# Summing the first values on VectorE instead of TensorE, and a tile's exponentials ahead of the weight decoding on ScalarE

## The chip, the cores and the metric

One NeuronCore of a Trainium2 chip runs the whole program. Five engines read instruction streams of their own, each in order: TensorE (PE, matmuls; PEld its weight loads), VectorE (DVE), ScalarE (ACT), GpSimd (POOL) and SyncE (SP, which issues the DMAs here). The metric is the device time of one execution in microseconds, the median of several runs. Less is better.

## The reference

Attention over pooled keys and values, then two feed-forward layers on its output of 4608 tokens by 512 (8 batches of 576 tokens; hidden width 2048; all float32).

```python
k_p = k.reshape(B, H, Sp, pool, D).mean(axis=3)      # B 8, H 8, Sp 72, pool 8, D 64
v_p = v.reshape(B, H, Sp, pool, D).mean(axis=3)
scores = scale * np.matmul(q, k_p.transpose(0, 1, 3, 2))
scores = scores - np.max(scores, axis=-1, keepdims=True)
attn = np.exp(scores)
attn = attn / (np.sum(attn, axis=-1, keepdims=True) + 1e-09)
x = np.matmul(attn, v_p)                             # then to (4608, 512)
...
h = x @ w_in                                         # layer 1
x2 = (h * np.clip(h + 3.0, 0.0, 6.0) / 6.0) @ w_out
h = x2 @ w_in2                                       # layer 2: a rational function of h, then
out = g @ w_out2
```

The weights are handed over as the 64-bit words of float64, and the kernel decodes them on the chip.

## The kernel before

**Slots.** The program is one list of slots, written out by `slot(s)`. Slots -12 to -1 are the prologue; slots 0 to 143 each compute one of the 16 hidden blocks of one of 9 token groups of layer 1 (`hidden`, 12 matmuls into `ps_h`), slots 144 to 287 the same of layer 2. The output matmuls of a block (`out1`, 12 matmuls into `ps_y`) come two slots later. The attention of the next token group is spread over the slots of the present one. Every instruction stands on its engine in the order in which `slot` writes it; nothing reorders it later.

**Layer 1 between the two matmuls.** `hard_swish_a` writes tile `r` on ACT from `ps_h` (L453) and finishes it on DVE (L454). `hard_swish_b`, at the start of the next slot, splits it: `gh` on ACT (L460) and `gl` on POOL (L461). There is one buffer of `r`, two each of `gh`, `gl` and `ps_h`.

**Attention of a tile of up to 128 queries.** Scores on PE into a PSUM bank `ps_s` (L333); the highest score on DVE, `nm` (L348); the exponentials on ACT (L355, four L358, L361), which read the bank for the last time; the reciprocal `rc` on DVE (L369); `s` scaled on POOL (L370, L376); transposes on PE (L385); `pth` and `ptl` (L396, L397); and after a group of tiles the product with the values, `ps_v` (L414). From the second token group on, scores, transposes and products take turns in two banks, `a0` and `a1`, so each waits for the last reader of what stood in the bank two turns ago. The highest score of a tile is written in the slot `s_s` of its scores; its exponentials (the list `ex`) in slot `s_s + 1`, right behind `hidden`.

**Weights.** A chunk of 128 by 512 weights is decoded by `decode_a` and `decode_r` on ACT (L154, L159), `decode_b` on DVE (L173, L174 into `t`) and `decode_c` on POOL (L181), and then split in two parts: the high part on ACT (`w`, L201), the low part, which reads the high one, on DVE or, for every fourth chunk, on POOL (L203). One chunk is decoded in a prologue slot, three in two slots from slot 0 on; the 32 chunks of layer 1 are done in slot 14. Within a slot the lists come as `c2` (split), `c1` (decode_b and c, from chunk 24 on the whole of a chunk), `c3` (decode_a and r of a chunk of the next slot), `la`.

**Values.** `v` comes as 6 chunks of 128 rows by 8 times 64, to be summed over the 8. For batch 0 that is `pool_first_v`: eight matmuls a chunk with the identity, into one bank, two chunks a slot in slots -11 to -9; the tiles are named after their buffers, so the first is `k_raw`. For the other batches it is `pool_v` on DVE (L248). `split_v` then makes `vsh` on ACT (L287) and the rest on DVE (L288), and POOL masks them (L297).

```python
        for h in ahead(s):
            hidden(h)
        for f in ex.get(s, ()):
            f()
        if 0 <= s - 1 < T1:
            hard_swish_b(s - 1)
...
        for kind in (c2, c1, c3, la):
            for f in kind.get(s, ()):
                f()
```

Of the kernel before, what the change touches and what calls it, by code (L numbers as in the profile page):

```python
# [19 lines left out]
F32 = mybir.dt.float32  # L20
# [4 lines left out]
AF = mybir.ActivationFunctionType  # L25
ALU = mybir.AluOpType
AX = mybir.AxisListType

B, H, S, D = 8, 8, 576, 64
POOLED = 8  # L30
SP = S // POOLED
NT, DM, DFF = B * S, H * D, 2048
P = 128
# [8 lines left out]
VCH = 6  # L42
# [26 lines left out]
def feed_forward_kernel(tc, q_t, k_t, v_r, vmask, w_in1, w_out1, w_in2, w_out2, a_rep, b_rep, out):  # L69
    nc = tc.nc  # L70
# [7 lines left out]
    att = tc.alloc_tile_pool(name="att", bufs=1, side="right")  # L78
    dram = tc.alloc_tile_pool(name="spill", bufs=1, space=bass.MemoryType.DRAM)
    ps_y = tc.alloc_tile_pool(name="ps_y", bufs=1, space=bass.MemoryType.PSUM)  # L80
# [7 lines left out]
    ident = const.tile([P, P], F32, name="ident")  # L88
# [153 lines left out]
    vsum = {}  # L242
# [23 lines left out]
            dst = kbd[rows, :, j, SM:SP] if p == NPAIR else kbd[rows, p, j, 0:SM]  # L266
            nc.vector.tensor_reduce(out=dst, in_=k[rows], axis=AX.X, op=ALU.add)

    def pool_first_v(c):
        if c == 0:  # L270
            vsum[0] = ps_y.tile([P, 512], F32, tag="y0", name="ps_vs")
        for r in range(POOLED):
            nc.tensor.matmul(
                vsum[0][:, c * D:(c + 1) * D], lhsT=ident, rhs=v_raw[0, c][:, r, :],
                start=r == 0, stop=r == POOLED - 1,
            )

    vparts = {}

    def split_v(b):  # L280
        src = vsum.pop(b)
        vs = src
        if b == 0:
            src = src[:, 0:VCH * D].rearrange("p (c d) -> p c d", d=D)
            vs = att.tile([P, VCH, D], F32, tag="vsum", name="vsum")
        vsh = att.tile([P, VCH, D], F32R, tag="vsh", name="vsh")
        nc.scalar.activation(out=vsh, in_=src, func=AF.Copy)  # L287
        nc.vector.tensor_tensor(  # L288
            out=vs[:, 0:4, :], in0=src[:, 0:4, :], in1=vsh[:, 0:4, :].bitcast(F32), op=ALU.subtract
        )  # L290
        vparts[b] = vsh.bitcast(F32), vs, src

    def mask_v(b, f, part):
        src, dst, nm = vparts[b][part], (vh, vl)[part], ("vh", "vl")[part]
# [9 lines left out]

    def mask_rest(b):

        hi, vs, src = (x[:, 4:6, :] for x in vparts[b])
        nc.vector.tensor_scalar(out=hi, in0=hi, scalar1=mask[:, 3:4], scalar2=None, op0=ALU.mult)
        nc.vector.scalar_tensor_tensor(
            out=vs, in0=src, scalar=mask[:, 2:3], in1=hi, op0=ALU.mult, op1=ALU.add  # L310
        )
        for i in range(2):
            nc.vector.tensor_scalar(
                out=vr[:, :, i, 1, :], in0=vs, scalar1=mask[:, 4 + i:5 + i], scalar2=None, op0=ALU.mult
            )
# [253 lines left out]
    def at(kind, slot, f, *a):  # L569
        kind.setdefault(slot, []).append(lambda: f(*a))  # L570
# [5 lines left out]
    def prepare_first(s0, units):  # L576

        at(dm, s0, load_q, *units[0])
        for p in (0, 1, NPAIR):
            at(dm, s0, load_first_k, p)  # L580
        at(dm, s0, load_weights, 0, *chunks[0])
        for u in units[1:3]:
            at(dm, s0, load_q, *u)
        for p in (2, 3):
            at(dm, s0, load_first_k, p)
        for c in range(VCH):
            at(dm, s0, load_v, 0, c)
            at(pe, s0 + 1 + c // 2, pool_first_v, c)
        at(dm, s0, load_weights, 0, *chunks[1])
        for p in (0, NPAIR, 1):  # L590
            at(el, s0, pool_first_k, p)
        for p in (2, 3):
            at(la, s0 + p - 2, pool_first_k, p)
        at(la, s0 + 3, split_v, 0)
        for i in range(4):
            at(la, s0 + 4 + i // 2, mask_v, 0, i // 2, i % 2)
        at(la, s0 + 4, mask_rest, 0)
# [19 lines left out]
    for j in range(NB):  # L617
        s0 = MF * (j - 1)
        tail, head = ([(b, g, f, ti) for f in range(2) for ti in GROUPS[b][g][2]] if 0 <= b < B else []
                      for b, g in ((j - 1, 1), (j, 0)))  # L620
        units = tail + head
        groups = [[u for u in units if u[0::2] == k] for k in dict.fromkeys(u[0::2] for u in units)]
        steps = len(units) + len(groups)
        k, done, last_s = 0, {}, {}
        for us in groups:
            b, g, f, _ = us[0]
            for u in us + [None]:
                s = s0 + round(14 * k / (steps - 1)) if j else k + 2 - PRE
                k += 1
                if u is None:  # L630
                    done[b, f] = s
                    for i in range(2):
                        at(pe, s, attend, b, g, f, i)
                        at(mid, s, split_x, b, g, 2 * f + i)
                    continue
                ti = u[3]
                s_t.append(s)
                s_s = s_t[-3] if len(s_t) > 2 else len(s_t) - 1 - PRE
                last_s[b, f] = s_s
                if len(s_t) > 3:  # L640
                    at(dm, s_s - 2, load_q, *u)
                at(pe, s_s, scores, *u)
                at(hi, s_s, highest, b, f, ti)
                at(ex, s_s + 1, exponentials, b, f, ti)
                at(nz, s_s + 1, normalize, b, f, ti)
                at(pe, s, transposes, *u)
                at(mid, s, split_p, *u)
        if j == 0:
            prepare_first(-PRE, units)
        elif head:  # L650
            k0 = last_s[j - 1, 0] + 1
            k1 = max(last_s[j - 1, 1] + 1, k0 + 2)
            a0 = max(done[j - 1, 0], done[j, 0] - 4)
            a1 = max(done[j - 1, 1], done[j, 0] - 3)
            prepare(j, k0, k1, a0, a1)
# [72 lines left out]
    def slot(s):  # L728
        d = s - LAG
        if s < 0:  # L730
            for kind in (dm, ld, el, pe, hi, ex, nz, c1, mid, c2, c3, la):
                for f in kind.get(s, ()):
                    f()
            return
        for f in dm.get(s, ()):
            f()
        for h in ahead(s):
            hidden(h)
        for f in ex.get(s, ()):
            f()  # L740
        if 0 <= s - 1 < T1:
            hard_swish_b(s - 1)
        for kind in (el, ld, pe):
            for f in kind.get(s, ()):
                f()
        if T1 <= s < T2:
            rational_a(s)
        if d > T1 and d % MF == 0:
            evac2((d - T1) // MF - 1)
        if 0 <= d < T1:  # L750
            out1(d)
        elif T1 <= d < T2:
            out2(d)
        for kind in (nz, mid, hi):
            for f in kind.get(s, ()):
                f()
        if 0 <= s < T1:
            hard_swish_a(s)
        if 0 <= d < T1 and d % MF == MF - 1:
            evac1(d // MF)  # L760
        if T1 <= s - 1 < T2:
            rational_c(s - 1)
        for kind in (c2, c1, c3, la):
            for f in kind.get(s, ()):
                f()
        if d == T1 - 1:
            to_second_left()
        if T1 <= s < T2:
            rational_b(s)
# [73 lines left out]
```

## Time and profile before

| | |
|---|---|
| three runs | 1771.32, 1772.97, 1776.14 us; median 1772.97 us |
| the profiled execution | 1775.16 us, of which its span 1773.4 us |
| busy share of the span | PE 97%, PEld 80%, ACT 56%, DVE 55%, POOL 51% |
| chain that ended last | PE 89% (L447 42%, L552 22%, L472 21%, L333 2%, L414 2%, L385 1%) |
| mean granted TensorE clock | 0.986 of full |

The span is the time from the first to the last instruction of the core; the 1.8 us beside it lie around the program. A busy share says how long an engine had work; which engine the others wait for is read from the rows of the stretch in question, with the idle time in front of an instruction and what ended it.

### The profile page before, as it was taken

To read this page: it belongs to the slowest core of one execution; us is meant where nothing else is said; L and a number is where in the kernel's file an instruction comes from. 1 tells how busy PE (TensorE), PEld (TensorE's weight loads), DVE (VectorE), ACT (ScalarE), POOL (GpSimd) and SP (SyncE) were. 2 spreads that over 40 slices of the span, in tenths; PEclk is the share of its full clock that TensorE was granted. 3 is DMA by queue.
4 is the path that set the end of the run, shared out by engine and by line. 5 is a ranking of instruction groups with operands and counts; after the bars stand their busy time and mean duration, and the time that the engine had idled before them with its cause. 6 is when DMAs were issued, how large, how long until landed. Compare 5 with 4: busy or idle time off the path is not lost.

```text
span 1773.4 us, 22277 instructions
## 1 busy us (share of the span) xinstructions
PE 1722.7 (97%) x7824; PEld 1426.9 (80%) x7824; DVE 982.8 (55%) x1617; ACT 992.6 (56%) x2226; POOL 907.8 (51%) x888
## 2 busy tenths in 40 slices
PE   6697999999999999999999999999999999999999
PEld 6575888888888888888888888888888888888887
DVE  5874534536354453533211566666666666666665
ACT  5765445555555454545322566666666666666665
POOL 3564333434334343433223666666666666666665
PEclk9798999999999999999999999999999999999999
DMA  6541303323232323312045301010101010101000
GB/s 206 165 137 58 107 20 114 114 83 132 77 131 91 123 85 105 117 66 87 12 149 208 113 13 41 7 42 7 42 7 42 7 42 7 42 7 42 1 24 25
DMA packets 68336, 128.33 MB, mean 72 GB/s; under 512 B 11392, under 2 KB 27776, under 8 KB 68224
## 3 DMA queue, kind: packets, MB, share of 16 engines
q1 hardware_dynamic: 68224, 126.91, 21.5%
q8 instruction: 62, 1.02, 0.2%
q14 instruction: 50, 0.41, 0.1%
HBM read 91.23 MB, written 35.65 MB: 72 GB/s over the span
## 4 chain that ended last, share of the span: by engine, by line
PE 89%; DVE 0%; ACT 0%; POOL 0%; issue 0%; DVEq 0%
PE ps_h L447 42%; PE ps_o L552 22%; PE ps_y L472 21%; PE ps_s L333 2%; PE ps_v L414 2%; PE ps_t L385 1%; ACT s L358 0%; POOL gl L538 0%; DVE t L514 0%; DVE g L529 0%; DVE r L525 0%; DVE qd L522 0%; DVE t L513 0%; ACT y L478 0%; ACT o L560 0%
## 5 line engine op out<-in xcount | busy, mean ns | idle before, releaser
L461 POOL TENSOR_TENSOR gl<-r,gh 128x512 fp32r<-128x512 f32 x144 | 186.9, 1298 | 470.3 <-ACT gh L460 463.4
L472 PE MATMUL ps_y<-gh,w 128*128 128x512 f32 x1152 | 393.4, 403 | 0.0
L447 PE MATMUL ps_h<-xh,w 128*128 128x512 f32 x1152 | 378.9, 390 | 0.0
L447 PE MATMUL ps_h<-x2h,w 128*128 128x512 f32 x1152 | 377.8, 389 | 0.8 <-DVE t L514 0.8
L552 PE MATMUL ps_o<-w,gh 128*128 128x512 f32 x1152 | 354.6, 389 | 0.0
L472 PEld LDWEIGHTS ps_y<-gh,w 128*128 128x128 f32 x1152 | 220.0, 191 | 47.4 <-issue 1.6
L447 PEld LDWEIGHTS ps_h<-x2h,w 128*128 128x128 f32 x1152 | 216.4, 188 | 46.3 <-DVE t L514 1.2
L447 PEld LDWEIGHTS ps_h<-xh,w 128*128 128x128 f32 x1152 | 216.5, 188 | 45.1
L552 PEld LDWEIGHTS ps_o<-w,gh 128*128 128x128 f32 x1152 | 216.2, 188 | 44.9
L509 POOL TENSOR_SCALAR qd<-ah,coef 128x512 f32<-128x512 f32 x144 | 111.4, 774 | 234.1 <-ACT ah L507 234.1
L472 PE MATMUL ps_y<-gl,w 128*128 128x512 f32 x576 | 227.4, 395 | 0.0
L447 PE MATMUL ps_h<-xl,w 128*128 128x512 f32 x576 | 224.1, 389 | 0.0
L447 PE MATMUL ps_h<-x2l,w 128*128 128x512 f32 x576 | 224.1, 389 | 0.0
L552 PE MATMUL ps_o<-w,gl 128*128 128x512 f32 x576 | 224.1, 389 | 0.0
L522 DVE SCALAR_TENSOR_TENSOR qd<-qd,r 128x512 f32<-128x512 f32 x144 | 99.0, 687 | 220.1 <-ACT r L521 203.8
L538 POOL TENSOR_TENSOR gl<-g,gh 128x512 fp32r<-128x512 f32 x144 | 186.4, 1295 | 19.2 <-ACT gh L537 19.0
L512 POOL TENSOR_TENSOR qd<-qd,ah 128x512 f32<-128x512 f32 x144 | 187.0, 1299 | 12.0
L454 DVE SCALAR_TENSOR_TENSOR r<-r,ps_h 128x512 f32<-128x512 f32 x144 | 99.0, 688 | 169.6 <-ACT r L453 167.1
L507 ACT ACTIVATE ah<-ps_h 128x512 f32<-128x512 f32 x144 | 86.1, 598 | 152.0 <-PE ps_h L447 152.0
L453 ACT ACTIVATE r<-ps_h,cst 128x512 f32<-128x512 f32 x144 | 98.7, 685 | 111.0 <-PE ps_h L447 76.3
L520 ACT ACTIVATE r<-qd,cst 128x512 f32<-128x512 f32 x144 | 99.6, 692 | 105.0 <-POOL qd L512 104.9
L460 ACT ACTIVATE gh<-r 128x512 fp32r<-128x512 f32 x144 | 90.1, 625 | 104.4 <-PE ps_y L472 101.9
(87 smaller groups left out, 2575.9 us busy)
## 6 DMA issues: line engine op xcount, KB each, us to landing
raw<-w_in SPq DMA_DIRECT2D x32, 512.0 KB, 3.7
raw<-w_out SPq DMA_DIRECT2D x32, 512.0 KB, 3.7
w<-raw SPq DMA_DIRECT2D x32, 512.0 KB, 2.8
w<-w SPq DMA_DIRECT2D x32, 512.0 KB, 4.1
v_raw<-v_r SPq DMA_DIRECT2D x47, 256.0 KB, 4.0
y<-y SPq DMA_DIRECT2D x36, 256.0 KB, 2.9
x2r<-y SPq DMA_DIRECT2D x36, 256.0 KB, 2.9
out<-o SPq DMA_DIRECT2D x36, 256.0 KB, 2.2
```

The source lines that it names most:

```text
L447: nc.tensor.matmul(ps, lhsT=w, rhs=x, start=o == 0, stop=o == len(ops) - 1)
L453: nc.scalar.activation(out=r, in_=ps, func=AF.Relu, bias=cst[:, 0:1], scale=1.0 / 6.0)
L454: nc.vector.scalar_tensor_tensor(out=r, in0=r, scalar=1.0, in1=ps, op0=ALU.min, op1=ALU.mult)
L460: nc.scalar.activation(out=gh[it], in_=r, func=AF.Copy)
L461: nc.gpsimd.tensor_tensor(out=gl[it], in0=r, in1=gh[it].bitcast(F32), op=ALU.subtract)
L472: nc.tensor.matmul(yp[j][c], lhsT=w, rhs=x, start=m == 0 and o == 0, stop=m == MF - 1 and o == 2)
L509: nc.gpsimd.tensor_scalar(out=qd, in0=ah, scalar1=absb[1], scalar2=absb[0], op0=ALU.mult, op1=ALU.add)
L512: nc.gpsimd.tensor_tensor(out=qd, in0=qd, in1=ah, op=ALU.mult)
L520: nc.scalar.activation(out=r0, in_=qd, func=AF.Ln, scale=2.0 ** -LN_SHIFT, bias=cst[:, 1:2])
L522: nc.vector.scalar_tensor_tensor(out=qd, in0=qd, scalar=1.0 + 1e-6, in1=r0, op0=ALU.add, op1=ALU.mult)
L538: nc.gpsimd.tensor_tensor(out=gl[it], in0=g, in1=gh[it].bitcast(F32), op=ALU.subtract)
L552: nc.tensor.matmul(yp[j][c], lhsT=w, rhs=x, start=m == 0 and o == 0, stop=m == MF - 1 and o == 2)
```

## The change

Two parts. The values of batch 0 are summed by `pool_v` on VectorE, as those of the other batches are: six reductions written at the end of slots -11, -10 and -9, two in each; `pool_first_v` with its 48 matmuls is gone, and `split_v` and `mask_rest` read the sums from SBUF instead of a PSUM bank. And the exponentials of a tile whose scores are in slot 0 or later are written at the end of that same slot, ahead of the lists `c2`, `c1`, `c3` and `la`, instead of in the next slot behind `hidden`. In the prologue they stay where they were.

```diff
-    def pool_first_v(c):
-        if c == 0:
-            vsum[0] = ps_y.tile([P, 512], F32, tag="y0", name="ps_vs")
-        for r in range(POOLED):
-            nc.tensor.matmul(
-                vsum[0][:, c * D:(c + 1) * D], lhsT=ident, rhs=v_raw[0, c][:, r, :],
-                start=r == 0, stop=r == POOLED - 1,
-            )
...
     def split_v(b):
-        src = vsum.pop(b)
-        vs = src
-        if b == 0:
-            src = src[:, 0:VCH * D].rearrange("p (c d) -> p c d", d=D)
-            vs = att.tile([P, VCH, D], F32, tag="vsum", name="vsum")
+        vs = vsum.pop(b)
...
-            at(pe, s0 + 1 + c // 2, pool_first_v, c)
+            at(la, s0 + 1 + c // 2, pool_v, 0, c)
...
-                at(ex, s_s + 1, exponentials, b, f, ti)
+                at(ex, s_s if s_s >= 0 else s_s + 1, exponentials, b, f, ti)
...
         for h in ahead(s):
             hidden(h)
-        for f in ex.get(s, ()):
-            f()
...
-        for kind in (c2, c1, c3, la):
+        for kind in (ex, c2, c1, c3, la):
             for f in kind.get(s, ()):
                 f()
```

`pool_v` itself is not changed:

```python
    def pool_v(b, c):
        if c == 0:
            vsum[b] = att.tile([P, VCH, D], F32, tag="vsum", name="vsum")
        vr = v_raw.pop((b, c)).rearrange("p r d -> p d r")
        nc.vector.tensor_reduce(out=vsum[b][:, c, :], in_=vr, axis=AX.X, op=ALU.add)
```

Where it moves rows (the changed kernel is shorter, so its L320 is the old L333, and so on), first on PE in the prologue. Before, from the first scores on (`ps_vs` are the sums of the values):

```order
L333 MATMUL ps_s<-kbd,q_sb 128x144 x4
L273 MATMUL ps_vs<-k_raw,ident 128x64 x8
L273 MATMUL ps_vs<-v_raw,ident 128x64 x8
L385 MATMUL ps_t<-ident,s 128x128 x3
L333 MATMUL ps_s<-kbd,q_sb 128x144 x2
L273 MATMUL ps_vs<-v_raw,ident 128x64 x16
L385 MATMUL ps_t<-ident,s 128x128 x3
```

And after:

```order
L320 MATMUL ps_s<-kbd,q_sb 128x144 x4
L372 MATMUL ps_t<-ident,s 128x128 x3
L320 MATMUL ps_s<-kbd,q_sb 128x144 x2
L372 MATMUL ps_t<-ident,s 128x128 x3
L320 MATMUL ps_s<-kbd,q_sb 128x144 x2
```

The 48 matmuls are gone, and the transposes and scores of the prologue follow each other directly.

On DVE the same sums come in, here those of slots -11 and -10, after the change:

```order
L174 SCALAR_TENSOR_TENSOR t<-d,t 128x512
L248 TENSOR_REDUCE vsum<-k_raw 128x64
L248 TENSOR_REDUCE vsum<-v_raw 128x64
L267 TENSOR_REDUCE kbd<-k_raw 64x64 x2
L335 TENSOR_REDUCE nm<-ps_s 128x4
L356 RECIPROCAL rc<-sm 128x4
L173 TENSOR_SCALAR t<-d 128x512
L174 SCALAR_TENSOR_TENSOR t<-d,t 128x512
L384 TENSOR_TENSOR ptl<-ps_t,pth 128x2x128
L388 TENSOR_TENSOR pth<-ps_t,pth 32x128
L203 TENSOR_TENSOR w<-t,w 128x512
L248 TENSOR_REDUCE vsum<-v_raw 128x64 x2
```

Before, the same rows stand there without the three of L248: two reductions have come in behind the decoding of slot -11, two behind the split of slot -10, and two more (not shown) behind that of slot -9.

The second part, on ACT in slot 2 (`raw` is a chunk of weights being decoded). Before:

```order
L453 ACTIVATE r<-ps_h,cst 128x512
L201 ACTIVATE w<-t 128x512
L154 ACTIVATE raw_673<-raw_673 128x512
L159 ACTIVATE raw_673<-raw_673 128x512
L355 ACTIVATE nm<-nm 128x4
L358 ACTIVATE s,sm<-ps_s,nm 128x72 x4
L361 ACTIVATE sm<-sm,cst 128x4
L460 ACTIVATE gh<-r 128x512
```

And after:

```order
L440 ACTIVATE r<-ps_h,cst 128x512
L342 ACTIVATE nm<-nm 128x4
L345 ACTIVATE s,sm<-ps_s,nm 128x72 x4
L348 ACTIVATE sm<-sm,cst 128x4
L201 ACTIVATE w<-t 128x512
L154 ACTIVATE raw_630<-raw_630 128x512
L159 ACTIVATE raw_630<-raw_630 128x512
L447 ACTIVATE gh<-r 128x512
```

The exponentials and the weight work have changed places between `r` and `gh`. The same exchange stands in slots 0, 4, 5, 6, 8, 10, 11, 12 and 13, and later with the one or two instructions for the weights of layer 2; slots 1, 3, 7, 9 and 14 have no exponentials. On PE nothing else moves, on DVE nothing but the six reductions, and the rows of POOL and of SP are the same in both.

## Rows read from the trace of the kernel before

**Rows 1.** Busy time of each engine in two stretches, from the first hidden block on: from:to, length, then busy us (and instructions) of PE, PEld, DVE, ACT and POOL, the granted TensorE clock, the DMA share and GB/s.

```profile
67.80:187.80 120.00, 100.74 (x432) 81.54 (x431) 82.11 (x143) 76.52 (x213) 65.30 (x65) 0.90 0.32 104
187.80:1773.40 1585.60, 1581.20 (x7219) 1309.66 (x7217) 854.95 (x1389) 874.74 (x1869) 812.53 (x777) 1.00 0.20 65
```

**Rows 2.** What PE waited for between 67 and 200 us: us in total, times, the longest.

```profile
PE ps_v L414 <- ACT s L358: 9.1, 3, 5.8
PE ps_s L333 <- ACT s L358: 8.0, 3, 4.0
```

**Rows 3.** The same list for all engines, between 67 and 200 us.

```profile
ACT r L453 <- POOL gl L461: 27.0, 12, 4.9
DVE w L203 <- ACT w L201: 7.8, 7, 2.2
```

**Rows 4.** Slot 2 in order of time, on ACT, then DVE, then POOL: start, duration, engine, line, operation; in brackets the idle time before it and what ended it. The last row of ACT is the `r` of slot 3.

```profile
88.52 0.69 ACT L453 ACTIVATE r<-ps_h,cst 128x512 f32<-128x512 f32 x1 [2.14 <-POOL gl L461]
89.11 0.62 ACT L201 ACTIVATE w<-t 128x512 fp32r<-128x512 f32 x1
90.74 0.19 ACT L355 ACTIVATE nm<-nm 128x4 f32<-128x4 f32 x1
92.52 0.61 ACT L460 ACTIVATE gh<-r 128x512 fp32r<-128x512 f32 x1
96.28 0.69 ACT L453 ACTIVATE r<-ps_h,cst 128x512 f32<-128x512 f32 x1 [2.62 <-POOL gl L461]
...
89.85 0.69 DVE L203 TENSOR_TENSOR w<-t,w 128x512 fp32r<-128x512 f32 x1
91.97 1.66 DVE L174 SCALAR_TENSOR_TENSOR t<-raw,t 128x512 int32<-128x512 int32 x1
...
93.71 1.30 POOL L181 TENSOR_TENSOR t<-t,raw 128x512 int32<-128x512 int32 x1 [0.63 <-DVE t L174]
94.97 1.28 POOL L461 TENSOR_TENSOR gl<-r,gh 128x512 fp32r<-128x512 f32 x1
```

**Rows 5.** Slot 0 in the same view, ACT and DVE.

```profile
71.48 0.68 ACT L453 ACTIVATE r<-ps_h,cst 128x512 f32<-128x512 f32 x1
72.05 0.63 ACT L201 ACTIVATE w<-t 128x512 fp32r<-128x512 f32 x1
74.59 0.20 ACT L355 ACTIVATE nm<-nm 128x4 f32<-128x4 f32 x1 [0.78 <-DVE nm L348]
...
75.19 0.68 DVE L203 TENSOR_TENSOR w<-t,w 128x512 fp32r<-128x512 f32 x1
```

**Rows 6.** The same view of the end of slot 5 (the `gl` on POOL) and of slot 6 (a split on POOL, and decode_b on DVE), then `gl` of slot 9 and `r` of slot 10.

```profile
117.73 1.30 POOL L461 TENSOR_TENSOR gl<-r,gh 128x512 fp32r<-128x512 f32 x1 [0.37 <-ACT gh L460]
120.35 1.29 POOL L203 TENSOR_TENSOR w<-t,w 128x512 fp32r<-128x512 f32 x1 [0.23 <-ACT w L201]
...
120.39 1.54 DVE L173 TENSOR_SCALAR t<-raw 128x512 int32<-128x512 int32 x1
...
149.64 1.28 POOL L461 TENSOR_TENSOR gl<-r,gh 128x512 fp32r<-128x512 f32 x1
...
151.24 0.68 ACT L453 ACTIVATE r<-ps_h,cst 128x512 f32<-128x512 f32 x1
```

**Rows 7.** The same view of slots 12 and 13 on ACT (`r` and exponentials of slot 12; `r` and exponentials of slot 13), and on PE the scores of slot 13, the second product of slot 14 and the first `out1` matmul of block 13 (slot 15).

```profile
169.90 0.69 ACT L453 ACTIVATE r<-ps_h,cst 128x512 f32<-128x512 f32 x1 [1.90 <-POOL gl L461]
176.13 0.19 ACT L355 ACTIVATE nm<-nm 128x4 f32<-128x4 f32 x1
180.83 0.69 ACT L453 ACTIVATE r<-ps_h,cst 128x512 f32<-128x512 f32 x1 [2.10 <-POOL gl L461]
183.04 0.20 ACT L355 ACTIVATE nm<-nm 128x4 f32<-128x4 f32 x1
...
177.72 1.33 PE L333 MATMUL ps_s<-kbd,q_sb 128*128 128x144 f32 x4 [3.95 <-ACT s L358]
186.00 0.37 PE L414 MATMUL ps_v<-pth,vh 128*128 128x448 f32 x1
192.30 0.39 PE L472 MATMUL ps_y<-gh,w 128*128 128x512 f32 x1
```

**Rows 8.** Two lines of the program over the whole span: durations (min/median/max in ns), first and last start, shapes. First the matmuls that sum the values, without those of the first chunk, then the sums of the values of the other batches on DVE.

```profile
L273 PE MATMUL ps_vs<-v_raw,ident x80: 275/421/421, 15.6 to 33.1; 128*128 128x64 f32 x80
L248 DVE TENSOR_REDUCE vsum<-v_raw x42: 1031/1076/1116, 72.5 to 747.8; 128x64 f32<-128x512 f32 x42
```

**Rows 9.** The prologue in order of time: on DVE the end of decode_b of slot -11, then the reciprocal and the split of slot -10; on ACT the end of the exponentials of slot -10, and `vsh` of slot -9.

```profile
14.00 0.69 DVE L174 SCALAR_TENSOR_TENSOR t<-d,t 128x512 int32<-128x512 int32 x1
21.30 0.18 DVE L369 RECIPROCAL rc<-sm 128x4 f32<-128x4 f32 x1
23.44 1.26 DVE L203 TENSOR_TENSOR w<-t,w 128x512 fp32r<-128x512 f32 x1
...
19.28 0.30 ACT L361 ACTIVATE sm<-sm,cst 128x4 f32<-128x4 f32 x1
33.39 0.49 ACT L287 ACTIVATE vsh<-ps_vs 128x384 fp32r<-128x384 f32 x1 [3.11 <-PE ps_vs L273]
```

**Rows 10.** The stretch right after PE's wait in slot 3, in the columns of rows 1.

```profile
92.30:97.40 5.10, 5.06 (x14) 4.19 (x15) 3.03 (x6) 2.27 (x7) 4.34 (x5) 0.50 0.57 180
```

**Rows 11.** All that PE waited for from 340 us to the end.

```profile
PE ps_h L447 <- DVE t L514: 0.8, 1, 0.8
```

More of the change, by code (lines that the diff above doesn't have):

```diff
@@ L267, in pool_first_k @@
             nc.vector.tensor_reduce(out=dst, in_=k[rows], axis=AX.X, op=ALU.add)
-    def pool_first_v(c):
-        if c == 0:
-            vsum[0] = ps_y.tile([P, 512], F32, tag="y0", name="ps_vs")
-        for r in range(POOLED):
-            nc.tensor.matmul(
-                vsum[0][:, c * D:(c + 1) * D], lhsT=ident, rhs=v_raw[0, c][:, r, :],
-                start=r == 0, stop=r == POOLED - 1,
-            )
     vparts = {}
     def split_v(b):
-        src = vsum.pop(b)
-        vs = src
-        if b == 0:
-            src = src[:, 0:VCH * D].rearrange("p (c d) -> p c d", d=D)
-            vs = att.tile([P, VCH, D], F32, tag="vsum", name="vsum")
+        vs = vsum.pop(b)
         vsh = att.tile([P, VCH, D], F32R, tag="vsh", name="vsh")
-        nc.scalar.activation(out=vsh, in_=src, func=AF.Copy)
+        nc.scalar.activation(out=vsh, in_=vs, func=AF.Copy)
         nc.vector.tensor_tensor(
-            out=vs[:, 0:4, :], in0=src[:, 0:4, :], in1=vsh[:, 0:4, :].bitcast(F32), op=ALU.subtract
+            out=vs[:, 0:4, :], in0=vs[:, 0:4, :], in1=vsh[:, 0:4, :].bitcast(F32), op=ALU.subtract
         )
-        vparts[b] = vsh.bitcast(F32), vs, src
+        vparts[b] = vsh.bitcast(F32), vs
     def mask_v(b, f, part):
@@ L305, in mask_rest @@
     def mask_rest(b):
-        hi, vs, src = (x[:, 4:6, :] for x in vparts[b])
+        hi, vs = (x[:, 4:6, :] for x in vparts[b])
         nc.vector.tensor_scalar(out=hi, in0=hi, scalar1=mask[:, 3:4], scalar2=None, op0=ALU.mult)
         nc.vector.scalar_tensor_tensor(
-            out=vs, in0=src, scalar=mask[:, 2:3], in1=hi, op0=ALU.mult, op1=ALU.add
+            out=vs, in0=vs, scalar=mask[:, 2:3], in1=hi, op0=ALU.mult, op1=ALU.add
         )
```

## The prediction

> **What bounds the kernel now.** I begin with the windows [rows 1]. From 187.8 us to the end PE is busy 1581 of 1585.6 us at a granted clock of 1.00, and after 340 us it waits 0.8 us in all [rows 11]. That stretch is PE's own work, and neither part of the change takes anything out of it. So the end moves by as much as the moment moves at which PE stops waiting. From 67.8 to 187.8 us PE is idle for 19.3 us, and the clock is 0.90.
>
> What PE waits for there are the exponentials: six waits, 17.1 us [rows 2]. A score, a transpose or a product needs one of two PSUM banks, and the exponentials read a bank last. It would be easy to stop at this list. But the list of all engines [rows 3] has a longer wait: ACT stands 27.0 us, in 12 of the slots, in front of `r` until POOL is through with the `gl` of the slot before, since `r` has one buffer. `r` starts right as `gl` ends: slot 2's `gl` runs from 94.97 to 96.25, slot 3's `r` starts at 96.28 [rows 4]. So slots 0 to 13 run around a **loop** that has nothing of PE in it: `r` on ACT, the high part `w` on ACT, the low part on DVE (L203), decode_b on DVE (last L174 at 91.97, for 1.66), decode_c on POOL (L181 at 93.71), `gl`, the next `r`. In slot 2 it takes 96.28 - 88.52 = 7.76 us. PE needs less: 186.00 to 192.30 is four product matmuls and the twelve each of `out1` and `hidden`, 6.3 us at full clock [rows 7]. So it has time to spare and waits for exponentials because it runs ahead of the loop.
>
> **Part one, the sums of the values.** PE loses 48 matmuls, each two records of about 0.42 us in the trace, the last starting at 33.1 [rows 8]. They stand on the path: `vsh` at 33.39 waits 3.11 us for them [rows 9], and ACT works on from there to the first block. DVE gets six reductions. It has 42 of the same shape, of 1.03 to 1.12 us [rows 8], 6.5 us for six. They go into DVE's stream, so I follow that. decode_b of slot -11 ends at 14.6 [rows 9]; two reductions and the keys' two (1.4) bring it to 18.1. There it waits for the exponentials of slot -10, which end at 19.6; these don't move, since nothing ahead of them on ACT does. From the reciprocal to the end of the split took 21.30 to 24.6, 3.3 us, and takes that again: 22.9. Two reductions and a maximum (0.45): 25.5. Slot -9 again 3.3, then two reductions: 30.95. `vsh` can start there, against 33.39: a gain of **2.4 us**, and the chain behind it moves with it. No DMA stands against that, for nothing of SP moves. The bounds: with six of the shortest reductions, 0.3 less, and two splits that meet no work of POOL (0.69 as in slot 2 instead of 1.26) [rows 4, 9], 1.1 less: a gain of 4 at best. If three of the six were stretched beside POOL as an L174 is (1.66 against 0.69) [rows 4, 9], 3 us more, and nothing is gained. I take 2.4, by the row of the same operation.
>
> **Part two, the exponentials first.** The block from `nm` to `sm` holds ACT for 92.52 - 90.74 = 1.78 us [rows 4]. It goes ahead of `w`, which is in the loop, and `gh`, at the end of both orders, is no earlier for it. In slot 2 DVE reaches L203 at 89.85 with `w` just done (89.11 + 0.62 = 89.73). Behind the exponentials `w` ends at 91.51, so L203, decode_b, decode_c, `gl` and the next `r` are all 1.7 us later. Queued behind the waiting L203 on DVE is all of decode_b; POOL's L181 waits for that, and `gl` stands behind L181. Slot by slot:
> - Slot 0: ACT would wait for `nm` until 74.59, so `w` goes from 72.05 to 76.4, and L203 from 75.19 to 77.1 [rows 5]: 1.9.
> - Slots 2 and 4: 1.7 each.
> - Slot 5: 1.7, less the 0.37 for which `gl` waited for `gh` [rows 6]: 1.3.
> - Slot 6: the split is POOL's (120.35), and DVE's decode_b at 120.39 doesn't wait for `w`; its 1.54 beside POOL shows that it even lost time there [rows 6]: 0.
> - Slot 8: 1.7. Slot 9 has no exponentials, and `r` of slot 10 came at 151.24, 0.3 behind the end of `gl` (149.64 + 1.28) [rows 6], which is a cushion; with an allowance of 0.2 for the same in slot 9, together 1.2.
> - Slots 10, 11 and 12: 1.8 each. DVE (or POOL) already waits there for `w` (part of the 7.8 us of L203) [rows 3], so nothing cushions.
>
> The sum at `r` of slot 13 is 1.9 + 3.4 + 1.3 + 0 + 1.2 + 5.4 = **13.2 us** later.
>
> Against that stands what PE gets back. In slot 12 the bank came free only after the weight work: `r` 169.90, exponentials 176.13, PE at 177.72 [rows 7]. With the exponentials right behind `r` (0.59 later) PE would have had it 5.6 us sooner. But PE then meets the next wait: the second product of slot 14 (186.00) needs the bank of the scores of slot 13, and their exponentials can't start before `r` of slot 13. That is 180.83 + 13.2 + 0.6 = 194.6, and the bank is free 1.6 later, 196.2. From there PE has the 6.3 us named above to the first `out1` of block 13 (192.30 before) [rows 7]. After such a wait the clock is down: 0.50 granted, 1.2 GHz, for the 5 us behind the wait in slot 3 [rows 10]. What takes 5 us there takes 2.5 at full clock; I add a little less, 1.9, and PE is at that `out1` at 204.4, 12.1 us later. `gl` of block 13, with another 1.8 from slot 13, is ready at 202.7 and not last. From there on everything is PE's.
>
> From slot 16 on the exchange costs nothing: PE covers it. Were that cover gone, each of the later tiles would add up to 1.8 us.
>
> **The sum.** 12.1 - 2.4 = 9.7 us later. The profiled execution (1775.16 us, 1773.4 of it span) becomes 1784.9; it lay 2.2 above the median of 1772.97, so the forecast is **1782.7 us**, slower by 0.55%. Its own range: with half of the 1.7 to 1.8 in the four late slots with exponentials (8, 10, 11, 12), 3.3 less, and the gain of 4 from part one, 4.8 us (1777.8); with 1.8 in all nine slots and no gain from part one, 15.1 us (1788.1).
>
> **The rivals.**
> - *Faster: PE's bank waits are the limit.* If `r` came when PE wants it, each of the six waits would shrink by the weight work ahead of the exponentials, from 1.6 us (89.11 to 90.74) [rows 4] to 5.6 as in slot 12. I take five sixths of the 17.1 us [rows 2], 14.2; with part one 16.6: 1756.4 us. For it speaks that they are most of PE's idle 19.3 us [rows 1]. Against it speaks that PE's early bank doesn't bring `gl` earlier [rows 3, 4]. It decides once the exponentials stay off the loop, that is if L203 finds `w` done in time. The Trainium skill's "Perfetto Trace Analysis" (section Optimization Strategy) says that the same gap repeating on the engine that should be saturated can mean that SBUF or PSUM lacks room for the next tile. By that rule the banks are the loss and this rival holds; the trace has the gap of PE, but the longer wait of ACT beside it.
> - *No difference: the lengthening is smaller.* Where a slot decodes two chunks (0, 2, 4, 6, 8) the last L174 takes about 1.66 against 0.69, as POOL is at work beside it (slot 2) [rows 4, 9]. If the later start took DVE and POOL apart, some 1.0 us would come back five times, 9.7 - 5 = 4.7, and with the larger gain of part one 3.1: 1776.1. Against it: both wait for the same `w` and move together.
> - *The change doesn't do what it says.* The exponentials are written early but can wait for `nm` with the weight work behind them. Slot 0 has that in the sum. If the nine other slots waited 0.8 us too, as slot 0 does [rows 5], they would be 7 us worse: 1789.7. `nm` is there before `r` in the other slots, as DVE writes it before L454.
>
> **How the numbers follow.** A measurement of this kernel tells 0.3% (5.3 us) from no change. The forecast has 0.66, the faster rival 0.13, the one without difference 0.16, the last 0.05. Slower by over 0.3%: 0.71; within: 0.16; faster: 0.13. The range that leaves out the faster rival and the end of the last is 1772 to 1790; 1756.4 lies outside it.
>
> **What would show it.** In the profile after: the six waits of PE for exponentials up to slot 13 mostly gone, and a longer one near slot 14; ACT's `r` still waiting for `gl`; DVE's L203 waiting for `w` for some 12 us more than 7.8; slot 2 from `r` to `r` 9.5 us instead of 7.8, slot 3 as before; `vsh` at 31.0; the first `hidden` 2.4 us earlier; from 200 us on no change. I am wrong if slot 2 keeps its 7.8 us, or if `r` no longer waits for `gl`.

## The result and the profile after

| | before | after |
|---|---|---|
| median of 4 runs (lowest to highest) | 1772.74 us (1771.32 to 1776.14) | 1785.87 us (1784.69 to 1787.30) |
| profiled execution, its span | 1775.16, 1773.4 us | 1784.69, 1782.9 us |

The change makes the kernel slower: the ratio of the medians is 1.0072, with a 95% interval from 1.0054 to 1.0089. The two profiled executions differ by 9.5 us, the medians by 13.1. In the changed kernel most lines of the program stand 13 lower: `r` is L440 and L441, `gl` L448, `nm` L342 and the exponentials L345; the weight lines L154 to L203 keep their numbers.

The windows of the profile after, in the stretches of [rows 1]:

```profile
67.80:187.80 120.00, 98.51 (x411) 76.98 (x410) 71.01 (x125) 67.97 (x191) 57.30 (x56) 0.90 0.29 94
187.80:1782.90 1595.10, 1586.92 (x7230) 1313.76 (x7230) 866.01 (x1404) 878.58 (x1886) 818.92 (x783) 1.00 0.20 65
```

At 187.8 us PE is now not yet past its waits: the second stretch is 9.5 us longer and has 11 PE instructions more. What all engines waited for between 67 and 200 us, against [rows 3]; the last line is ACT's wait for the highest score:

```profile
ACT r L440 <- POOL gl L448: 49.4, 14, 5.0
...
DVE w L203 <- ACT w L201: 22.0, 12, 2.7
...
ACT nm L342 <- DVE nm L335: 1.1, 1, 1.1
```

And PE alone in the same stretch, the whole list, against [rows 2]:

```profile
PE ps_s L320 <- ACT s L345: 6.3, 4, 3.2
PE ps_y L459 <- POOL gl L448: 4.3, 3, 2.9
PE ps_t L372 <- DVE xl L413: 4.0, 1, 4.0
PE ps_v L401 <- DVE pth L388: 3.8, 1, 3.8
PE ps_t L372 <- POOL s L363: 3.8, 1, 3.8
PE ps_v L401 <- ACT s L345: 2.0, 3, 0.8
PE ps_t L372 <- DVE pth L388: 0.5, 1, 0.5
```

PE's waits for exponentials fell from 17.1 to 8.3 us, and the kernel got slower. What PE gained there it lost elsewhere: its waits for `gl`, `xl`, `pth` and `s` are 16.4 us (before, 2.1, for `xl`), so that it stands 24.7 us in all instead of 19.2. ACT's wait for `gl` grew by 22.4 us and DVE's wait for `w` by 14.2. Slot 2 in order of time, as in [rows 4]:

```profile
87.08 0.69 ACT L440 ACTIVATE r<-ps_h,cst 128x512 f32<-128x512 f32 x1 [2.13 <-POOL gl L448]
87.67 0.20 ACT L342 ACTIVATE nm<-nm 128x4 f32<-128x4 f32 x1
...
89.45 0.61 ACT L201 ACTIVATE w<-t 128x512 fp32r<-128x512 f32 x1
...
91.10 0.61 ACT L447 ACTIVATE gh<-r 128x512 fp32r<-128x512 f32 x1
...
96.56 0.69 ACT L440 ACTIVATE r<-ps_h,cst 128x512 f32<-128x512 f32 x1 [4.63 <-POOL gl L448]
...
90.10 0.69 DVE L203 TENSOR_TENSOR w<-t,w 128x512 fp32r<-128x512 f32 x1 [1.60 <-ACT w L201]
...
92.23 1.68 DVE L174 SCALAR_TENSOR_TENSOR t<-raw,t 128x512 int32<-128x512 int32 x1
...
93.98 1.30 POOL L181 TENSOR_TENSOR t<-t,raw 128x512 int32<-128x512 int32 x1 [0.63 <-DVE t L174]
95.24 1.28 POOL L448 TENSOR_TENSOR gl<-r,gh 128x512 fp32r<-128x512 f32 x1
```

The block from `nm` to `w` takes 89.45 - 87.67 = 1.78 us; DVE now waits 1.60 for `w`, and from `r` to `r` it is 9.48 us instead of 7.76. `gh` is done long before POOL comes to `gl`. The end of the stretch, slots 12 to 15, on ACT and then PE, as in [rows 7]:

```profile
178.07 0.69 ACT L440 ACTIVATE r<-ps_h,cst 128x512 f32<-128x512 f32 x1 [4.37 <-POOL gl L448]
...
190.78 0.69 ACT L440 ACTIVATE r<-ps_h,cst 128x512 f32<-128x512 f32 x1 [3.85 <-POOL gl L448]
...
199.52 0.69 ACT L440 ACTIVATE r<-ps_h,cst 128x512 f32<-128x512 f32 x1 [3.27 <-POOL gl L448]
...
190.29 0.71 PE L401 MATMUL ps_v<-pth,vh 128*128 128x448 f32 x1 [3.79 <-DVE pth L388]
...
192.96 0.74 PE L401 MATMUL ps_v<-pth,vh 128*128 128x448 f32 x1 [0.84 <-ACT s L345]
...
201.01 0.39 PE L459 MATMUL ps_y<-gh,w 128*128 128x512 f32 x1
```

The first `out1` of block 13 moved from 192.30 to 201.01 us, 8.7 later. From there to the end it is 1581.9 us against 1581.1. All of PE's waits from 340 us on, as in [rows 11]:

```profile
PE ps_h L434 <- DVE t L501: 0.8, 1, 0.8
```

And `vsh`, whose sums now end on DVE, as in [rows 9]:

```profile
30.47 0.52 ACT L274 ACTIVATE vsh<-vsum 128x384 fp32r<-128x384 f32 x1 [5.19 <-DVE vsum L248]
```

### The profile page after: what moved, and what is told of

It reads as the page before. It is cut to its first block, busy times and chain, and to the rows that moved or that the text cites. A ratio compares the mean times of both kernels' runs of the same rounds, so it can differ in the third digit from the quotient of the medians.

```text
span 1782.9 us, 22092 instructions
## 1 busy us (share of the span) xinstructions
PE 1713.0 (96%) x7728; PEld 1411.9 (79%) x7728; DVE 991.4 (56%) x1623; ACT 989.9 (56%) x2226; POOL 908.0 (51%) x888
## 4 chain that ended last, share of the span: by engine, by line
PE 88%; DVE 1%; ACT 0%; POOL 0%; DMA 0%; issue 0%; DVEq 0%
PE ps_h L434 41%; PE ps_o L539 22%; PE ps_y L459 20%; PE ps_s L320 2%; PE ps_v L401 2%; PE ps_t L372 1%; ACT s L345 0%; DMA k_raw<-k_t 0%; DVE kbd L240 0%; DVE vsum L248 0%; POOL gl L525 0%; POOL t L181 0%; POOL gl L448 0%; ACT y L465 0%; DVE t L501 0%
## 5 line engine op out<-in xcount | busy, mean ns | idle before, releaser
L448 POOL TENSOR_TENSOR gl<-r,gh 128x512 fp32r<-128x512 f32 x144 | 186.4, 1295 | 453.0 <-ACT gh L447 446.8
L441 DVE SCALAR_TENSOR_TENSOR r<-r,ps_h 128x512 f32<-128x512 f32 x144 | 99.0, 687 | 175.7 <-ACT r L440 173.4
L440 ACT ACTIVATE r<-ps_h,cst 128x512 f32<-128x512 f32 x144 | 98.6, 685 | 137.2 <-POOL gl L448 71.0
```

The source lines that it names most:

```text
L440: nc.scalar.activation(out=r, in_=ps, func=AF.Relu, bias=cst[:, 0:1], scale=1.0 / 6.0)
L441: nc.vector.scalar_tensor_tensor(out=r, in0=r, scalar=1.0, in1=ps, op0=ALU.min, op1=ALU.mult)
L448: nc.gpsimd.tensor_tensor(out=gl[it], in0=r, in1=gh[it].bitcast(F32), op=ALU.subtract)
```

## The experiments

The theory was that of the prediction: slots 0 to 13 run round the loop (the expectations also say ring) `r`, `w`, L203, decode_b, decode_c, `gl`, next `r`, and what stands on ACT ahead of `w` is paid once per slot. The rivals were that PE's banks are the limit, and that exponentials cost their time on ACT wherever they stand. This table has, for all kernels, the time, the ratio to the kernel before on the same chip, and, from the starts of `r` in the trace, the time from `r` of slot 0 to `r` of slot 6 and from `r` of slot 10 to `r` of slot 14.

| kernel | median us | ratio, 95% interval | slots 0 to 6 | slots 10 to 14 |
|---|---|---|---|---|
| before | 1772.74 | | 47.6 | 36.5 |
| after | 1785.87 | 1.0054 to 1.0089 | 52.8 | 43.5 |
| e1 sums only | 1773.78 | 0.9990 to 1.0008 | 47.4 | 36.5 |
| e2 exponentials only | 1786.05 | 1.0051 to 1.0078 | 54.2 | 43.5 |
| e3 `w` first in slots 0 to 8 | 1779.36 | 1.0017 to 1.0037 | 48.2 | 43.5 |
| e4 `gh`, `gl` early | 1798.12 | 1.0119 to 1.0147 | 52.3 | 42.2 |
| e6 decode_c behind `gl`, exponentials first | 1783.45 | 1.0042 to 1.0076 | 52.4 | 43.5 |
| e7 the same, exponentials in the old place | 1772.27 | 0.9985 to 1.0003 | 46.0 | 36.5 |
| e8 exponentials first from slot 16 on | 1774.78 | 0.9999 to 1.0018 | 47.0 | 36.5 |
| e9 exponentials behind the decoding | 1775.36 | 0.9999 to 1.0018 | 47.6 | 36.6 |
| e10 low part behind decode_b | 1777.86 | 1.0013 to 1.0031 | 46.9 | 43.6 |
| e11 e9 and e10 together | 1774.04 | 0.9993 to 1.0012 | 46.9 | 36.5 |
| e12 decode_c behind `gl` in all slots | 1769.09 | 0.9952 to 0.9977 | 46.6 | 32.7 |

e1 to e4 shared a chip, whose runs of the kernel before had a median of 1773.59. In e5 to e8 it was 1773.29, in e9 to e11 1773.29, in e12 1775.79. So a difference of a few us between kernels of different groups is told by their ratios, not by their times.

**e1, the sums alone, and e2, the exponentials alone.** e1 takes from the diff all but the place of the exponentials, e2 only that place:

```diff
-                at(ex, s_s + 1, exponentials, b, f, ti)
+                at(ex, s_s if s_s >= 0 else s_s + 1, exponentials, b, f, ti)
...
-        for kind in (c2, c1, c3, la):
+        for kind in (ex, c2, c1, c3, la):
```

> Only part one: the values summed on VectorE, the exponentials where they were. Loop theory (the round from r over w, decode_b, decode_c and gl to the next r sets slots 0 to 13; the exponentials ahead of w lengthen it): vsh near 30.5 us as with the whole change, r of slot 0 some 2 us earlier than 71.5, and every later r by the same; 1771 us, 2 less than before. Rival (the six reductions cost DVE what PE saves, or keep it from the weights): 1773 or more.

> Only part two: the exponentials ahead of the weight work, the values still summed on PE. Loop theory: all of the loss is here, r of slot 13 some 12 us later than 180.8, 1786 to 1788 us. Rival (the loss is in both parts, DVE being short of time): a clear part of it missing, under 1782.

The whole loss is part two's: e2 is 12.5 us above the kernel before on its chip and 0.2 above the changed kernel. That was e2's forecast. e1 missed its 1771 us: the sums alone are worth nothing that can be measured, though `vsh` (31.72 us) and `r` of slot 0 (69.92) came earlier than in the profile of before.

**e3, `w` ahead of the exponentials.** Only the order of the lists changes. Up to slot 8 `c2` holds a `w`, later `w` is written in `c1`, so the edit reaches slots 0 to 8 alone.

```diff
-        for kind in (ex, c2, c1, c3, la):
+        for kind in (c2, ex, c1, c3, la):
```

> The whole change, but on ACT the split of the chunk before (list c2, the high part w) ahead of the exponentials, and only the decoding behind them. Loop theory: in slots 2, 4 and 5 w is not delayed any more, so their loops are as long as before the change; in slots 10 to 13, where the split stands in list c1, the 1.8 us a slot stay. r of slot 13 about 6 us earlier than with the change; 1779 to 1781 us. Rival (ACT as a whole is too late with the weights, whatever the order of its pieces; or the earlier exponentials hurt PE): no different from the change, 1785 to 1787.

Slots 0 to 6 fell from 52.8 to 48.2 us, almost to the 47.6 of before, and slots 10 to 14, where the order is untouched, kept 43.5. The time is 6.5 us below the changed kernel's, as forecast. It is the place on ACT relative to `w` that counts, with the exponentials still at the end of the slot of their scores.

**e4, `gh` and `gl` right behind the hard swish.** This was to cut the loop, by writing `gh` and `gl` ahead of the weight work of their own slot.

```diff
-        if 0 <= s - 1 < T1:
-            hard_swish_b(s - 1)
...
             hard_swish_a(s)
+            hard_swish_b(s)
```

> The whole change, and gh and gl of a block written in its own slot right behind hard_swish_a, ahead of the exponentials and the weight work, so that gl no longer stands behind decode_c on POOL. Loop theory: the next r waits only for r, L454, gh and gl, some 3.5 us; PE sets the pace from slot 1 on, its waits for exponentials are under 5 us in all, ACT no longer waits for gl; r of slot 13 earlier than before the change by 10 us or more; 1752 to 1762 us. Rival (the decoding itself, 21 chunks in 14 slots on DVE and POOL, is what the slots last, and r's wait for gl only shows it): no faster than 1775 us, with PE waiting for weights or for attention instead.

It missed by far. The waits between 67 and 200 us:

```profile
ACT gh L447 <- DVE r L441: 47.8, 15, 5.3
DVE w L203 <- ACT w L201: 38.6, 14, 4.2
```

`gh` needs DVE's part of `r`, and standing right behind `r` on ACT it waits there for what DVE has queued, with exponentials and `w` behind it. So there was a new loop through L441 and `gh`, no shorter than the old one. It also costs after slot 16, where the other kernels lose nothing: from `r` of slot 16 to the end it is 1796.0 - 206.5 = 1589.5 us, against 1782.9 - 207.4 = 1575.5 in the changed kernel. PE's waits from 190 us on:

```profile
PE ps_s L320 <- ACT s L345: 6.6, 4, 2.9
PE ps_v L401 <- ACT s L345: 4.2, 3, 2.3
```

As an edit it moved too much at once, and it decides nothing between the theories. Its rival, that the decoding by itself is what the slots last, is answered by e12 below: the same decoding goes through slots 10 to 14 in 32.7 us there.

**e5, the kernel before once more.** No edit.

> The kernel before, profiled a second time. Its timed runs lie between 1771.3 and 1776.7; the first profiled one took 1775.2, above the median of 1773.6. If that one was merely late in its first 70 us, this one shows vsh still near 33.4 us but the hard swishes' r of slots 0 to 16 some 0 to 3 us earlier than 71.5 to 198.7 us, and 1771 to 1776 us in all, while the time behind r(16) stays at 1574.5 to 1575.5 us. If the 2 us of the first sums are a real gain of the changed kernel, r(0) stays at 71.0 to 71.5 us and only the time behind r(16) varies.

It took 1775.03 us; `vsh` came at 33.18 and `r` of slot 0 at 71.1 us. So the first profile of before was no accident of its own. But e2 has the same summing matmuls, and there `vsh` came 3.3 us earlier. The summing matmuls in e2, as in [rows 8], then its `vsh`:

```profile
L273 PE MATMUL ps_vs<-v_raw,ident x80: 219/275/421, 16.1 to 29.6; 128*128 128x64 f32 x80
...
29.91 0.49 ACT L287 ACTIVATE vsh<-ps_vs 128x384 fp32r<-128x384 f32 x1 [1.88 <-PE ps_vs L273]
```

The median duration is 275 ns there, 421 in both profiles of before; the last section shows what the two cases are. With the sums on DVE `vsh` came between 30.47 and 32.03 us in all eleven profiles: later than in the one of TensorE's two cases, earlier than in the other.

**e6 and e7, decode_c behind `gl`.** The part of the decoding on POOL goes into the next slot, behind `gl`; e6 has the exponentials in the new place, e7 in the old. (e7 has the sums on DVE; the expectation says TensorE.)

```diff
             at(c1, s, decode_b, *c)
-            at(c1, s, decode_c, *c)
+            at(*((dc, s + 1) if 0 <= s and i < 23 else (c1, s)), decode_c, *c)
...
             hard_swish_b(s - 1)
+        for f in dc.get(s, ()):
+            f()
```

> The changed kernel, but the GpSimd part of the weight decoding of slots 0 and later is put into the next slot, right behind that slot's gl on GpSimd, so that gl, which the next r waits for, no longer stands behind it: the ring r, w, DVE's low part, decode_b, decode_c, gl, r is cut, and the place of gh on ACT is untouched. Loop theory: r waits for gl far less than the 49 us of the changed kernel, and the time falls below that of the kernel before: 1752 to 1768 us. Rival (another ring of the same length takes its place, by DVE's two steps ahead of the min-multiply, or the exponentials cost their time on ACT wherever they stand): 1778 us or more.

> The same move of the GpSimd part of the decoding, on the kernel before (exponentials in their old place, first sums on TensorE). Loop theory: 1752 to 1768 us too, and the place of the exponentials is worth less than 4 us between this and the run with the exponentials ahead, where it is worth 12 with the ring whole. Rival (the exponentials' place costs by itself, not through the ring): this one is 9 us or more below that run. Rival (the waits for score banks are the limit): the run with the exponentials ahead is the faster one by 5 us or more.

Both missed, and the distance of 11.2 us between them is the one that the rival had named. Two things came together. The edit reached slots 0 to 7 alone, since from chunk 24 on the decoding is written in one piece: slots 10 to 14 stayed at 43.5 and 36.5. And in slots 0 to 6 it gained only 0.4 and 1.4 us against the same kernels without it (the changed one and e1). e7's waits between 67 and 200 us show why:

```profile
POOL gl L448 <- ACT gh L447: 22.4, 9, 6.5
ACT w L201 <- POOL t L181: 16.3, 15, 2.3
ACT r L440 <- POOL gl L448: 16.2, 12, 2.1
```

`gl` no longer waits behind decode_c, but for `gh`, which stands on ACT behind `w`, and `w` now waits for decode_c. With one loop cut the next, only little shorter, sets the pace: `r`, all that ACT has up to `gh`, `gl`, the next `r`. The exponentials lie on that one in either place, so their own time would cost the same in e6 and e7. What e6 pays beyond e7 in slots 0 to 6, 6.4 us, goes with another wait, that of ACT for `nm` in slots 0, 2, 4 and 5 of e6:

```profile
ACT nm L342 <- DVE nm L335: 8.1, 4, 2.7
```

In e7 it is 0.9 us in all. Ahead of `w` the exponentials come up before DVE has written `nm`, and `w` and `gh` wait with them; this is the mechanism of the prediction's last rival. In slots 10 to 14, which the edit didn't reach, the other 7.0 us stayed. The theory's step "with `gl` free of decode_c PE is the limit" fell. Whether the exponentials ahead of `w` lengthen the loop through decode_c these two runs don't decide; e9 and e10 do.

**e8, the new place from slot 16 on.**

```diff
-                at(ex, s_s + 1, exponentials, b, f, ti)
+                early_ex = 16 <= s_s < 1000
+                at(e0 if early_ex else ex, s_s if early_ex else s_s + 1, exponentials, b, f, ti)
...
-        for kind in (c2, c1, c3, la):
+        for kind in (e0, c2, c1, c3, la):
```

> The first sums as changed, and the exponentials ahead of the decoding only for tiles whose scores stand in slot 16 or later, so in nearly all tiles of the program but not in the slots of the ring. Loop theory: no cost, 1773 to 1775 us, as the sums alone (1773.8). Rival (each exponentials group ahead of w costs wherever it stands): 1780 us or more.

Most tiles of the program have the new place here, and the time is 1.5 us above the kernel before (the interval reaches to 3.2) and 1.0 above e1, as forecast: the loss is not per tile, but per slot of the loop.

**e9, exponentials behind the decoding.**

```diff
-        for kind in (ex, c2, c1, c3, la):
+        for kind in (c2, c1, ex, c3, la):
```

> The changed kernel, but the exponentials of a tile stand behind the weight decoding of their slot instead of ahead of it: still at the end of the slot of their scores, still ahead of the next slot's gh. The score banks come free 2 to 5 us later than in the changed kernel and still a slot's start earlier than in the kernel before. In the run with w ahead of the exponentials in slots 0 to 7 alone, r(0) to r(6) already fell from 52.8 to 48.2 us and the slots from 10 to 13 kept 12.8, 9.3, 12.7 and 8.7 us. Ring theory (what stands on ScalarE between r and the last w is paid, what stands behind it is not): slots 10 to 13 fall back to 11.0, 7.6, 10.9 and 7.0 us, 1773 to 1776 us in all. Rival (exponentials at the end of a slot cost because they stand ahead of gh there): 1779 us or more.

A hit, in the time and in the four slots. Slot 12 on ACT:

```profile
169.17 0.69 ACT L440 ACTIVATE r<-ps_h,cst 128x512 f32<-128x512 f32 x1 [1.91 <-POOL gl L448]
...
174.86 0.63 ACT L201 ACTIVATE w<-t 128x512 fp32r<-128x512 f32 x1 [2.25 <-POOL t L181]
175.40 0.19 ACT L342 ACTIVATE nm<-nm 128x4 f32<-128x4 f32 x1
...
177.18 0.61 ACT L447 ACTIVATE gh<-r 128x512 fp32r<-128x512 f32 x1
...
180.10 0.69 ACT L440 ACTIVATE r<-ps_h,cst 128x512 f32<-128x512 f32 x1 [2.10 <-POOL gl L448]
```

The same exponentials, still ahead of `gh`, now lie beside DVE's and POOL's decoding: 10.9 us from `r` to `r`, as before the change, against 12.7 with them ahead of `w`. One slot did not fall back: slot 5 takes 8.9 us in e3, e9, e10 and e11, against 8.1 with the exponentials in the old place. There they also come ahead of `vsh` of the next batch, which POOL's masks, ahead of `gl`, wait for; from e9:

```profile
POOL vh L284 <- ACT vsh L274: 1.1, 1, 1.1
```

**e10 and e11, DVE's low part behind decode_b.** L203 of a chunk is written behind decode_b of the next in slots 0 to 8, where `t` has buffers enough (`later` leaves that part of the split to `split_low`); e11 has e9's order as well.

```diff
-                at(c2, s + 1, split_weights, *c)
+                if s + 1 >= 0:
+                    at(c2, s + 1, lambda *x: split_weights(*x, later=True), *c)
+                    at(c4, s + 1, split_low, *c)
+                else:
+                    at(c2, s + 1, split_weights, *c)
...
-        for kind in (ex, c2, c1, c3, la):
+        for kind in (ex, c2, c1, c4, c3, la):
```

> The changed kernel with the exponentials in their new place ahead of w, but in slots 0 to 8 VectorE's low part of the split weights stands behind the shift and merge of the next chunk's decoding (these early chunks have t buffers of their own). So VectorE no longer waits for w ahead of that decoding, and the exponentials are off the ring there; from slot 9 on the order is as in the changed kernel. Ring theory: r(0) to r(6), 52.8 us in the changed kernel and 47.4 with the exponentials in their old place, is 48.5 us or less, slots 10 to 13 keep 12.8, 9.3, 12.7 and 8.7, and the time is 1774 to 1780 us. Rival (the exponentials cost by their work on ScalarE between r and gh, whatever VectorE does): r(0) to r(6) stays over 51 us, 1783 us or more.

> The two edits before this together: exponentials behind the decoding, VectorE's low part behind the next shift and merge in slots 0 to 8. Ring theory: r(0) to r(6) 47.5 us or less and slots 10 to 13 as in the kernel before: 1766 to 1775 us, the lowest of the three. Rival: as the exponentials behind the decoding alone, the low part's place being worth nothing once w comes early: within 1 us of that run.

e10 takes the link between `w` and decode_b away by writing the low part later, and leaves the exponentials ahead of `w` throughout. Slot 2 on ACT and DVE (the low part is L211 there, `r` L448 and L449):

```profile
85.95 0.69 ACT L448 ACTIVATE r<-ps_h,cst 128x512 f32<-128x512 f32 x1 [2.04 <-POOL gl L456]
...
88.32 0.62 ACT L201 ACTIVATE w<-t 128x512 fp32r<-128x512 f32 x1
...
93.53 0.69 ACT L448 ACTIVATE r<-ps_h,cst 128x512 f32<-128x512 f32 x1 [2.73 <-POOL gl L456]
...
87.28 0.42 DVE L173 TENSOR_SCALAR t<-raw 128x512 int32<-128x512 int32 x1
...
90.41 0.68 DVE L211 TENSOR_TENSOR w<-t,w 128x512 fp32r<-128x512 f32 x1
```

DVE starts decode_b at 87.28, before `w` has begun, and finds `w` done when it comes to the low part. The slot takes 7.58 us, with the exponentials in the new place. Slots 0 to 6 fell to 46.9 us, the late ones kept 43.6: the cost of 5 us in the first is gone, that of 7 in the last is there. This is the run that shows the loop, since the exponentials didn't move. Its two stretches and its time came as forecast. e11 has the same cut with the exponentials behind the decoding, and its slots 0 to 6 take the same 46.9 us: without the link their place is worth nothing there. In all, e11 fell into its range; being 1.3 us below e9, it doesn't tell whether the low part's place is worth anything beside that.

**e12, decode_c behind `gl` in all slots.** e7, with the same for the last chunk of each slot from slot 8 on:

```diff
             decode_b(0, *chunks[i])
-            decode_c(0, *chunks[i])
+            if slot_of(i + 1) > slot_of(i):
+                at(dc, slot_of(i) + 1, decode_c, 0, *chunks[i])
+            else:
+                decode_c(0, *chunks[i])
```

> The kernel before, with the GpSimd part of the decoding behind the next slot's gl in slots 0 to 7 (as run already: 1772.3 us, r(0) to r(6) 46.0 us) and now also, in the slots from 8 to 14, for the last chunk of each slot. There the next r no longer waits for VectorE's low part, shift and merge and GpSimd's add of that chunk, only for w, gh and gl. Ring theory, part on those four steps: r(7) to r(14), 61.4 us in that run, falls by 5 to 14 us until TensorE is the limit, 1760 to 1768 us in all. Rival (what ScalarE does between r and gh, and GpSimd's add ahead of the next w, make a ring about as long, as in slots 0 to 7): 1769 to 1773 us.

(e12 too has the sums on DVE.) The forecast missed, and the time is the rival's. Slots 10 to 14 fell from 36.5 to 32.7 us, slots 7 to 14 from e7's 61.4 to 58.2 (in e1, without the move, they take 59.0): the loop through decode_c did set the pace there, but the next one is only some 10% shorter. This is the one version that beats both kernels, by 0.35% against the kernel before on its chip, whose median was the highest of the four; against e1, which has the same sums but ran on another chip, it is 4.7 us. What now ends last, between 67 and 200 us:

```profile
POOL gl L448 <- ACT gh L447: 35.9, 14, 6.6
ACT w L201 <- POOL t L181: 16.7, 16, 2.3
ACT r L440 <- POOL gl L448: 12.5, 10, 1.7
```

## Why the prediction was right

- **What bounds the kernel.** Right, and shown: e3, e9 and e10 each take the exponentials off the loop in another way, in named slots, and the loss goes in those slots, but for 0.8 us of slot 5, and stays in the others. The rival on PE's banks is out: its waits for exponentials went from 17.1 to 8.3 us in the changed kernel, and the end came later. The hint cited from the Trainium skill ("Perfetto Trace Analysis", section Optimization Strategy), that such a repeated gap can mean a lack of room in PSUM, did not carry here: PE's gap was slack against the loop. The other two rivals are out by the rows above: L174 in slot 2 still took 1.68 us beside POOL (1.66 before), and ACT waited for `nm` once, 1.1 us.
- **Part two slot by slot.** At the starts of `r`, before and after, the slots became longer by 0.5 (slot 0; forecast 1.9), 1.72 (2; 1.7), 1.67 (4; 1.7), 1.27 (5; 1.3), 0.13 (6; 0), 1.4 (8 and 9; 1.2), and 1.74, 1.69 and 1.78 (10, 11, 12; 1.8 each). Together 11.9 of 13.2 us. The miss is slot 0 alone. There `nm` was ready at 71.29 us, 1.8 behind `r`; before, it was 3.1 behind it, since DVE had waited 0.59 us for a DMA and begun the keys' sums later. The prediction had taken that wait as it stood; in e2, where DVE waited 0.46 us for the DMA again, slot 0 grew by 2.0. In slot 5 the forecast price is right, but the path named is not the only one: without it, as in e9, 0.8 us stays by the road through `vsh`, which the prediction hadn't seen.
- **What PE meets next.** The second product of slot 14 waited for the exponentials of slot 13 as forecast, and stood at 192.96 (forecast 196.2 - 2.4 = 193.8). Ahead of it the first product waited 3.79 us for `pth`, which stands on DVE behind decode_b: the same loop by another road, which the prediction hadn't seen; the second product had to wait for the exponentials in any case. From 192.96 to `out1` of block 13 it took 8.05 us instead of 6.3, 1.75 more (forecast 1.9); the granted clock was 0.55 for the first half of it and 1.00 for the second.
- **The signs.** Slot 2 from `r` to `r` 9.5 us: 9.48. L203's wait for `w` some 12 us longer: 14.2. `r` still waiting for `gl`: 49.4 us. `vsh` at 31.0: 30.47. The first `hidden` 2.4 us earlier: 2.5. Two signs were off. PE's waits for exponentials were to be mostly gone, and 8.3 of 17.1 us stayed, with other waits of PE in place of the rest. And the longer wait of PE near slot 14 has two causes where one was named.
- **From slot 16 on nothing.** Right within what e8 can tell: 1.5 us, at most 3.2. In the two profiles 0.8 us came on top behind `out1` of block 13.
- **Part one, the term that was mis-sized.** Forecast was a gain of 2.4 us. In the two first profiles `vsh` came 2.9 earlier and `r` of slot 0 2.0; but the medians of e1 and of before are the same within 0.1%, and e2 and the changed kernel differ by 0.2 us. The prediction took the matmuls' 0.42 us [rows 8] as their price. That is the price at the slower of two paces of TensorE; in e2 the faster one set in some 8 us earlier, the median was 0.28, and TensorE was as early as DVE (last section). That the runs of before (1770.9 to 1776.7 us beside e1 to e8, where e1 lay within 1772.6 and 1775.1) are a mixture of both is argued, since the timed runs have no trace.
- **How the sum came out.** Against the profiled execution 9.7 was forecast and 9.5 measured. That it came so near is in part luck, since two errors cancel: part two was 12.5 us (e2) where 12.1 stood, part one nothing where -2.4 stood, and the two profiled executions lie apart less than the medians, as before's is 2.4 above its median and after's 1.2 below. So the median, 1785.87, is 3.2 above the forecast of 1782.7, within the range.

What stays open: whether the exponentials ahead of `w` would cost nothing beside e12's order in the late slots was not run, nor was the kernel with two buffers of `r`.

## What to carry to other kernels

When an engine of the loop waits for a buffer, follow the list of all engines round until it closes, and ask of each moved block whether it stands ahead of or behind the instruction that feeds the next engine: 1.78 us of ACT cost 1.7 a slot ahead of `w` and nothing behind it, but in slot 5, where a second road led to the same buffer. Before expecting a gain from cutting a loop, look for the next one through the same engines: here it was only some 10% shorter. And one profile of a kernel is one sample: a term of 2 us read from it needs a second.

## What the runs showed of the hardware

The summing matmuls (128x64, float32, the identity as weights) had a median of 421 ns in both profiles of before and of 275 in e2, with the same instructions ahead of them in the program; between 20 and 26 us PE started 30 instructions in the one case and 44 in the other. This is no matter of these matmuls. At one moment in the prologue all of PE's instructions go over to about twice the pace: at about 30 us in both profiles of before, at about 22 us in e2. PE had been busy almost without a break since 12 us in all three. Four records of the scores, in before, the first ahead of that moment, the second behind it, the third behind a wait of 3 us:

```profile
27.93 1.17 PE L333 MATMUL ps_s<-kbd,q_sb 128*128 128x144 f32 x4
...
33.53 0.66 PE L333 MATMUL ps_s<-kbd,q_sb 128*128 128x144 f32 x4
...
37.81 1.17 PE L333 MATMUL ps_s<-kbd,q_sb 128*128 128x144 f32 x4
```

And in e2:

```profile
20.15 1.17 PE L333 MATMUL ps_s<-kbd,q_sb 128*128 128x144 f32 x4
...
25.70 0.66 PE L333 MATMUL ps_s<-kbd,q_sb 128*128 128x144 f32 x4
```

The records of the summing matmuls start every 0.21 us ahead of that moment and every 0.11 behind it. In the row at 37.81 the granted clock is 0.50, the 1.2 GHz level. In the other four it reads 1.00, and yet the same work takes 1.17 us at 20.15 and 27.93, as at 0.50. So in these profiles a granted clock of 1.00 in the first 30 us doesn't tell PE's pace; the duration of a known instruction does. In e2 the moment came some 8 us earlier, and `vsh` 3.3 us. What sets the moment is open. The six reductions on DVE that took the matmuls' place took 996 to 1043 ns in the changed kernel.
